# Two head pairs' queries transposed by a DMA instead of TensorE, one copy for two pairs' keys, and a new order of work beside the units

## The chip, the cores and the metric

The kernel runs on one core of one Trainium2 chip. The metric is the device time of one execution in microseconds; several executions are timed and the median is given. One further execution is recorded by the hardware profiler.

## The reference

Inputs are q, k and v of shape (8 sequences, 8 heads, 576 positions, 64), a small position network (w1, b1, w2), and a mixture of eight experts.

```python
scores = q @ k^T / 8 + bias[h]            # per sequence and head; bias depends on position and head alone
attn   = exp(scores - max);  attn /= attn.sum(-1) + 1e-9
x      = attn @ v                          # -> (8*576 tokens, 512)
for e in range(8):                         # every token belongs to one expert (moe_domain_id)
    out[tokens of e] = relu(x[tokens of e] @ w1[e]) @ w2[e]     # 512 -> 1024 -> 512
```

## The kernel before, in words

**Stages.** A first stage evaluates the position network and leaves exp(bias) tables in SBUF (`_phase_bias`, nine blocks `ib` = 0 to 8). A second does the attention of the eight sequences (`_Attention.run`) and scatters the rows of x, sorted by expert, to a scratch tensor `fire_x` in HBM. A third runs the experts (`_phase_moe`). At the start of the first stage one SP DMA fills `fire_x` with zeros (line 277, 9252 KB).

**Attention of one sequence.** Scores are computed with the keys on the partitions. The eight heads are four pairs p = 0 to 3. A sequence has 21 *units*, each some matmuls into a PSUM tile `sc` (two buffers) and one exponential on ScalarE (`L593`) from there to SBUF: unit 0 `("r", 0)` and unit 9 `("r", 1)` hold the last 64 keys of pairs 0, 1 and of pairs 2, 3; units 1 to 8 the 512 main keys of pairs 0 and 1; 10 to 13 those of pair 2; 14, 15 the last 64 queries; 16 is a small corner (256 columns); 17 to 20 the main keys of pair 3. Unit 20 and its like add the bias by a matmul (`L561`); the others are multiplied by the exp(bias) tables on VectorE.

**Beside the units.** TensorE, VectorE and ScalarE each run in the order in which the program is written (`manual_schedule`). `PLAN` is that order: slot n of the list is put behind unit n. `A p c` is one group of attention-times-value matmuls of pair p (p = 4 is the last 64 queries) into the one PSUM tile `pu`; `N p` normalizes `pu` on VectorE (a reciprocal and a multiply) and must end before the next pair's first `A`; `W n` multiplies unit n's exponentials by their table; `V` copies v beside its columns of ones; `T p q` and `T p k` are eight TensorE transposes each for the next sequence's q and k of pair p into a PSUM tile `pt` (p = 4: the last 64 rows, four each); `D p` copies that tile to SBUF on VectorE. A prime means that the work belongs to the preceding sequence. `PLAN0` is the same list for sequence 0.

**Loads.** GpSimd issues the loads of q, k and v (float32 in HBM, float16 in SBUF) two sequences ahead, in a fixed order with the scatters (`G.issue`); `n4` is a ring of six buffers for them. q and k lie as [128, 8 heads, 4 rows, 64]: partition i holds positions 4i to 4i+3. SP issues the zero fill, the experts' transposing reads of `fire_x` (lines 830 and 993, `dma_start_transpose`) and their staged weights (786); its order is the tile framework's.

**Sequence 0.** Pairs 2 and 3 of sequence 0 are transposed after units 4 and 5 and copied out of PSUM by ScalarE (`L533`), one copy each. Behind unit 7 stand the transposes of the last 64 rows of sequence 1 (`T4q`, `T4k`, tile `last`).

**Into the experts.** When the first seven sequences are scattered, SP issues a transposing read `xA` of the first 512 rows of expert 0 (line 993). TensorE's first expert matmul (`L851`) stands behind the last `A` group of sequence 7.

Of the kernel before, what the change touches and what calls it, by code (L numbers as in the profile page):

```python
# [40 lines left out]
W4 = C4 + S  # L41
# [8 lines left out]


PLAN = (
    "A40' A41' A42'",
    "W19' A43' A44' A45' V",
    "A46' A47' W0",
    "T0q T0k N4'",
    "T4q W2 D0 A30' A31'",
    "A32' A33' A34'",
    "A35' A36' A37' W4",
    "T1q T4k",  # L60
    "N3' A00 A01 A02 D4",
    "W6 A03 W8 A04",
    "A05 A06 A07",
    "T2q",
    "T1k N0 A10",
    "W9 A11 A12 W11",
    "A13 A14 D1 A15",
    "A16 A17",
    "W13",
    "T2k N1",  # L70
    "D2 A20 A21 A22 A23 A24 A25 A26 A27 W15 N2",
    "",
    "T3q W18 T3k D3",
)

PLAN0 = [" ".join(t for t in slot.split() if t not in ("T0q", "T0k", "T4q", "D0")) for slot in PLAN]
# [21 lines left out]

def _ins(inst):
    return inst.ins if hasattr(inst, "ins") else inst  # L100


class _Issue:
# [94 lines left out]
def _phase_bias(tc, G, route, at, x_dram):  # L198


    nc = tc.nc
    with tc.tile_pool(name="fsb", bufs=1, side="right") as fsb, \
# [67 lines left out]
        for ib in range(9):  # L270
            if ib == 7:
                at.transposes(0, 1)
            after = hidden(ib + 1) if ib < 8 else None
            if ib == 1:
                G.last_table()
                nc.vector.memset(G.zero.rearrange("p o (r d) -> p (o r) d", r=4)[:, :, DM:].bitcast(I32), PAD)
                nc.sync.dma_start(out=x_dram.rearrange("(p c r) d -> p c (r d)", p=P, r=4),
                                  in_=G.zero.to_broadcast([P, NSLOT // P // 4, 4 * XW]))
            if ib == 5:
                at.transposes(0, 4)  # L280
                at.transposes(0, 0)
            if ib == 8:
                for ui in range(HEAD):
                    at.unit(0, ui, fps.tile([P, 2, 512], F32, tag="eb", name="eb", bufs=3))
            outputs(ib, hrl)
            if ib == 0:
                next(route)
            if ib == 8:
                at.weight(at.jobs.pop((0, 0)))
                at.make_vext(0)  # L290
                for k in range(7):
                    if k == 3:
                        at.weight(at.jobs.pop((0, 2)))
                    next(route)
            hrl = after
# [134 lines left out]
class _Attention:  # L430
# [10 lines left out]
    def __init__(self, tc, G, q, k, v, x_dram):  # L441
        self.tc, self.nc, self.G = tc, tc.nc, G
        self.q, self.k, self.v, self.x_dram = q, k, v, x_dram
        self.nat, self.vst, self.qkT, self.qkTl, self.e, self.xt, self.xl, self.pt = ({} for _ in range(8))
# [24 lines left out]
    def load_qk(self, b, xs="qk"):  # L469
        nc = self.nc  # L470
        for nm in xs:
            src = self.q if nm == "q" else self.k
            t = self.G.n4(nm + "n").rearrange("p (h r d) -> p h r d", r=4, d=D)
            self.G.issue(nc.gpsimd.dma_start(out=t, in_=src[b, :, 0:512, :]
                                        .rearrange("h (p r) d -> p h r d", r=4)))
            self.nat[b, nm] = t

    def load_last(self, b, xs="qk"):
        nc = self.nc
# [28 lines left out]
    def transposes(self, b, p, xs="qk"):  # L508

        G = self.G  # L510
        if "q" in xs:
            self.pt[b, p] = G.tps.tile([P, 2, 512] if p < 4 else [P, 4, 2, 128], F16, tag="tr",
                                       name="pt" if p < 4 else "ptl", bufs=2)
        pt = self.pt[b, p]
        for nm in xs:
            x = "qk".index(nm)
            for r in range(4):
                if p < 4:
                    for h2 in range(2):
                        self._transpose(pt[64 * h2: 64 * h2 + 64, x, 128 * r: 128 * r + 128],  # L520
                                        self.nat[b, nm][:, 2 * p + h2, r, :], 128)
                else:
                    self._transpose(pt[:, r, x, :], self.last[b % 2][:, r, x, :], 128)

    def take(self, b, p, eng=None):
        if p < 4:
            t = self.qkT[b, p] = self.G.asb.tile([P, 2, 512], F16, tag="qkT", name="qkT", bufs=8)
        else:
            t = self.qkTl[b] = self.G.asb.tile([P, 4, 2, 128], F16, tag="qkTl", name="qkTl", bufs=2)
        if eng is None:  # L530
            self.nc.vector.tensor_copy(out=t, in_=self.pt.pop((b, p)))
        else:
            eng.copy(out=t, in_=self.pt.pop((b, p)))  # L533

    def unit(self, b, ui, sc=None):
        self.jobs[b, ui] = self.scores(b, self.units[ui], sc)

    def scores(self, b, u, sc=None):
        nc, G = self.nc, self.G
        mm = nc.tensor.matmul  # L540
# [15 lines left out]
        if u[0] == "m":  # L556
# [4 lines left out]
                    mm(out=sc[:, h2, :], lhsT=G.idn, rhs=G.biasW[c][:, 2 * p + h2 - RAW[c], :],  # L561
                       start=True, stop=False)
            for h2 in range(2):
                mm(out=sc[:, h2, :], lhsT=self.qkT[b, p][hs[h2], 1, 128 * c: 128 * c + 128],  # L564
                   rhs=self.qkT[b, p][hs[h2], 0, :], start=not raw, stop=True)
            c0 = c if j is None else c - 1
            bias = None if raw else G.biasM[:, c0: c + 1, 2 * p: 2 * p + 2, :].rearrange("p c h i -> p c (h i)")
        elif u[0] == "r":
            for p in range(2):
                mm(out=sc[:, p, :], lhsT=self.qkTl[b][:, 2 * u[1] + p, 1, :],  # L570
                   rhs=self.qkT[b, 2 * u[1] + p][:, 0, :], start=True, stop=True)
            bias = G.biasR[:, 2 * u[1]: 2 * u[1] + 2, :].rearrange("p q i -> p (q i)")
        elif u[0] == "l":
            for lj in range(2):
                c = 2 * u[1] + lj
                for p in range(4):
                    mm(out=sc[:, lj, :].rearrange("k (h p q) -> k h p q", h=2, p=4)[:, :, p, :],
                       lhsT=self.qkT[b, p][:, 1, 128 * c: 128 * c + 128],
                       rhs=self.qkTl[b][:, p, 0, :].rearrange("k (h q) -> k h q", h=2),
                       start=True, stop=True)  # L580
# [12 lines left out]
        nc.scalar.activation(out=ef[:, 0:n], in_=sf[:, 0:n], func=AF.Exp, bias=0.0, scale=0.125)  # L593
        if bias is None or j == 0:
            return None
        if j == 1:
# [95 lines left out]
    def run(self, route, late):  # L692
# [338 lines left out]
```

## Time and profile before

| | us |
|---|---|
| time, median of 3 runs (lowest to highest) | 355.24 (354.95 to 355.83) |
| the profiled execution's own time | 355.02 |
| its span, first to last instruction | 353.5 |
| TensorE matmul busy in the span | 324.5 (92%) |
| VectorE busy | 247.3 (70%) |
| ScalarE busy | 246.3 (70%) |
| GpSimd busy | 167.7 (47%) |

The span lacks some 1.5 us of the execution's own time. The busy shares are means over three stages: the position network to about 50 us, attention to about 207 us, the experts behind it. A matmul's end is modelled, so a busy TensorE may also be waiting inside a group. Two neighbouring instructions' records overlap a little, so a pace is read from start to start.

### The profile page before, as it was taken

The numbers are of one execution on the slowest core, as the hardware profiler recorded it, in microseconds if no ns is written. First come the engines' busy times: TensorE is split into PE (matmuls) and PEld (weight loads), VectorE is DVE, ScalarE is ACT, GpSimd is POOL, SyncE is SP. The second block draws the span as 40 slices with busy tenths as digits, with TensorE's granted clock in tenths as the row PEclk, the third lists the DMA queues.
The fourth block names the chain that finished last, engine by engine and source line by source line (L and its number), as shares of the span: only waits on it lengthen the run. The fifth ranks groups of instructions, "written<-read, shape, count | busy, mean of one in ns | idle before, by whom it ended". The sixth has DMA issues, their size and how long they took to land. (4 is left out here: it accounts for less than half of the span.)

```text
span 353.5 us, 9881 instructions
## 1 busy us (share of the span) xinstructions
PE 324.5 (92%) x4218; PEld 213.4 (60%) x4218; DVE 247.3 (70%) x436; ACT 246.3 (70%) x299; POOL 167.7 (47%) x211
## 2 busy tenths in 40 slices
PE   0489888999999999999999899999999999999993
PEld 0478855766666676666675564565655555565651
DVE  7999998999999999999999861206163616161211
ACT  7999989999999999999999953241424232323330
POOL 8370004727687676958483622506051515151323
PEclk9999757999999999999999999999999999999998
DMA  3999999999999899999999543999999999980202
GB/s 43 195 158 345 352 341 213 192 194 163 167 128 192 115 190 111 200 101 200 149 202 220 129 71 93 283 323 230 322 206 325 248 289 264 271 322 32 114 32 107
DMA packets 89349, 69.20 MB, mean 196 GB/s; under 512 B 43605, under 2 KB 77653, under 8 KB 89304
## 3 DMA queue, kind: packets, MB, share of 16 engines
q0 software_dynamic: 51984, 37.26, 65.0%
q1 hardware_dynamic: 37320, 31.30, 32.7%
q8 instruction: 33, 0.54, 0.6%
q14 instruction: 12, 0.10, 0.1%
HBM read 61.93 MB, written 24.70 MB: 245 GB/s over the span
## 5 line engine op out<-in xcount | busy, mean ns | idle before, releaser
L593 ACT ACTIVATE e<-sc 128x1024 f16<-128x1024 f32 x157 | 148.2, 1059 | 1.7
L874 ACT ACTIVATE hT<-hps 128x640 f16<-128x640 f32 x56 | 39.4, 704 | 78.1 <-PE hps L841 77.8
L820 DVE COPY res<-ops 128x512 f32<-128x512 f32 x39 | 27.0, 692 | 91.1 <-PE ops L813 90.1
L821 POOL DMA_INDIRECT out_dram<-res,ids x40 | 44.9, 1123 | 89.8 <-DVE res L820 73.3
L604 DVE TENSOR_TENSOR e<-e,biasM 128x2048 f16<-128x2048 f16 x64 | 72.9, 1149 | 1.6 <-ACT e L593 1.5
L813 PE MATMUL ops<-w,hT 128*128 128x512 f16 x320 | 70.5, 379 | 0.0
L629 PE MATMUL pu<-vext,e 128*128 128x65 f16 (+1 forms) x1280 | 64.8, 194 | 0.0
L841 PE MATMUL hps<-xT,w 128*128 128x320 f16 x448 | 62.0, 299 | 0.0
L629 PEld LDWEIGHTS <-e 128*128 128x128 f16 (+1 forms) x1280 | 56.1, 101 | 8.8 <-issue 6.8
L841 PEld LDWEIGHTS <-w 128*128 128x128 f16 x448 | 43.8, 98 | 18.1
L813 PEld LDWEIGHTS <-hT 128*128 128x128 f16 x320 | 31.2, 98 | 36.5 <-ACT hT L853 0.3
L564 PE MATMUL sc<-qkT 64*128 64x512 f16 x252 | 49.7, 391 | 3.8 <-ACT e L593 3.6
L671 POOL DMA_INDIRECT fire_x<-xt,posi x32 | 40.1, 1253 | 15.3 <-issue 7.6
L218 DVE TENSOR_SCALAR hr<-L,slope,nb 128x576 f16<-128x576 f16 x113 | 41.4, 433 | 0.1
L238 PE MATMUL eb<-W2BIG,hr 128*128 128x32 f16 x576 | 24.0, 192 | 14.6 <-DVE W2BIG L187 10.1
L627 PE MATMUL pu<-vrag,e 128*128 128x130 f16 (+1 forms) x160 | 35.7, 223 | 0.2 <-ACT e L593 0.2
L238 PEld LDWEIGHTS <-hr 128*128 128x128 f16 x576 | 21.5, 115 | 17.8 <-POOL vrag L450 6.7
L215 ACT ACTIVATE hr<-L,pb,slope 128x576 f16<-128x576 f16 x31 | 24.6, 873 | 1.4 <-DVE nb L183 1.2
L671 POOL DMA_INDIRECT fire_x<-xl,posi x8 | 9.1, 1133 | 30.8 <-issue 13.8
L564 PEld LDWEIGHTS <-qkT 64*128 64x128 f16 x256 | 13.5, 93 | 16.3 <-issue 8.3
L643 DVE TENSOR_TENSOR xt<-pu,rz 128x512 f16<-128x512 f32 (+1 forms) x33 | 22.3, 675 | 1.5
L627 PEld LDWEIGHTS <-e 128*128 128x128 f16 (+1 forms) x160 | 16.0, 100 | 11.2 <-issue 6.6
(124 smaller groups left out, 352.5 us busy)
## 6 DMA issues: line engine op xcount, KB each, us to landing
st<-in_moe_w_dram SPq DMA_DIRECT2D x15, 1024.0 KB
fire_x<-zero SPq DMA_DIRECT2D x1, 9252.0 KB
w<-in_moe_w_dram POOLq DMA_DIRECT2D x17, 512.0 KB
qn<-in_q_dram POOLq DMA_DIRECT2D x8, 512.0 KB
kn<-in_k_dram POOLq DMA_DIRECT2D x8, 512.0 KB
vst<-in_v_dram POOLq DMA_DIRECT2D x8, 512.0 KB
out_dram<-res,ids POOLq DMA_INDIRECT x40
last<-zero SPq DMA_DIRECT2D x2, 256.0 KB
```

The costliest lines, as they stand in the source:

```text
L218: nc.vector.tensor_scalar(out=hr, in0=G.L4[:, c0: c0 + S], scalar1=G.slope[:, m: m + 1], scalar2=G.nb1[:], op0=AO.mult, op1=AO.max)
L238: nc.tensor.matmul(out=eb[:, lj, 32 * k16: 32 * k16 + 32], lhsT=rap(hr, jc, [[4, 128]]), rhs=G.W2BIG[:, 0:32], start=True, stop=True)
L564: mm(out=sc[:, h2, :], lhsT=self.qkT[b, p][hs[h2], 1, 128 * c: 128 * c + 128], rhs=self.qkT[b, p][hs[h2], 0, :], start=not raw, stop=True)
L593: nc.scalar.activation(out=ef[:, 0:n], in_=sf[:, 0:n], func=AF.Exp, bias=0.0, scale=0.125)
L604: self.nc.vector.tensor_tensor(out=job[0], in0=job[0], in1=job[1], op=AO.mult)
L627: mm(out=out, lhsT=last, rhs=vr[:, pair, :], start=True, stop=False, skip_group_check=True)
L629: mm(out=out[:, 65 * h2: 65 * h2 + 65], lhsT=keys[j], rhs=vx[:, 2 * pair + h2, j, :], start=False, stop=(h2 == 1 and j == 3), skip_group_c ...
L671: inst = self.nc.gpsimd.indirect_dma_start(out=self.x_dram[:, :], out_offset=bass.IndirectOffsetOnAxis(ap=self.G.posi[0:n, c:c + 1], axis= ...
L813: nc.tensor.matmul(out=ops_, lhsT=hT[:, fc, t0: t0 + 128], rhs=G.w.w2(e, fc), start=(fc == 0), stop=(fc == 7))
L821: inst = nc.gpsimd.indirect_dma_start(out=out[:], out_offset=bass.IndirectOffsetOnAxis(ap=idx.bitcast(I32), axis=0), in_=res[:], in_offset ...
L841: nc.tensor.matmul(out=hps[:, i, 0:HC], lhsT=G.w.w1(e, dc, fc), rhs=xT[:, dc, HC * hf: HC * hf + HC], start=(dc == 0), stop=(dc == 3))
L874: nc.scalar.activation(out=hT[:, fc, :].rearrange("p (a b) -> p a b", a=2), in_=first(e, xT, ((fc, 0), (fc, 1))), func=AF.Relu, bias=0.0, ...
```

## The change

`load_qk` loads q in two DMAs: heads 0 to 3 into the first half of the buffer as before, and heads 4 to 7 into its second half, `natx`, a [128, 1024] block. A new function `cross` issues one transposing DMA on SP from `natx` to a new tile `qx` (two buffers). For sequence 0 it is called in block 4 of the first stage without a further wait; for sequence b + 1 it is called behind unit 4 of sequence b and waits, by a semaphore (`_behind`), for that unit's exponential. The transposes `T2q` and `T3q` are gone; `T2k` and `T3k` write the two halves of one PSUM tile, and one copy `D2` moves both (`D3` is gone). In sequence 0 one ScalarE copy stands behind unit 4 where two stood behind units 4 and 5. The matmuls take q of pairs 2 and 3 from `qx` and k of both from one tile. `PLAN` is dealt anew.

```diff
-    "A40' A41' A42'",            "W19' A43' A44' A45' V",     "A46' A47' W0",
-    "T0q T0k N4'",               "T4q W2 D0 A30' A31'",       "A32' A33' A34'",
-    "A35' A36' A37' W4",         "T1q T4k",                   "N3' A00 A01 A02 D4",
-    "W6 A03 W8 A04",             "A05 A06 A07",               "T2q",
-    "T1k N0 A10",                "W9 A11 A12 W11",            "A13 A14 D1 A15",
-    "A16 A17",                   "W13",                       "T2k N1",
-    "D2 A20 A21 A22 A23 A24 A25 A26 A27 W15 N2",  "",         "T3q W18 T3k D3",
+    "W18' A40' A41' A42' V T0q", "A43' A44' A45' W0",         "A46' A47' W19'",
+    "N4' T0k",                   "W2 A30' A31' T4q",          "D0 A32' A33' A34'",
+    "A35' W4 A36' A37'",         "T4k T1q",                   "N3' A00 W6 D4 A01",
+    "A02 A03 A04 W8",            "W9 A05 A06",                "A07 N0 T2k",
+    "T1k",                       "A10 A11 A12",               "A13 A14 D1 W11 A15",
+    "W13 A16 A17 N1",            "",                          "T3k D2",
+    "A20 W15 A21 A22 A23 A24 A25",  "A26 A27",                "N2",
...
+            if ib == 4:
+                at.cross(0)
...
-            t = self.G.n4(nm + "n").rearrange("p (h r d) -> p h r d", r=4, d=D)
-            self.G.issue(nc.gpsimd.dma_start(out=t, in_=src[b, :, 0:512, :]
+            src = (self.q if nm == "q" else self.k)[b, :, 0:512, :]
+            t = self.G.n4(nm + "n")
+            n = 1024 if nm == "q" else 2048
+            self.nat[b, nm] = t[:, 0:n].rearrange("p (h r d) -> p h r d", r=4, d=D)
+            self.G.issue(nc.gpsimd.dma_start(out=self.nat[b, nm], in_=src[0: n // 256]
                                         .rearrange("h (p r) d -> p h r d", r=4)))
+            if nm == "q":
+                self.natx[b] = t[:, n:]
+                self.G.issue(nc.gpsimd.dma_start(out=t[:, n:].rearrange("p (r h d) -> p r h d", r=4, d=D),
+                                                 in_=src[4:].rearrange("h (p r) d -> p h r d", r=4)))
+    def cross(self, b, behind=None):
+        self.qx[b] = self.G.asb.tile([P, 4, 2, 128], F16, tag="qx", name="qx", bufs=2)
+        inst = self.nc.sync.dma_start_transpose(out=self.qx[b].rearrange("p r a i -> p (r a) i"),
+                                                in_=self.natx.pop(b))
+        if behind is not None:
+            _behind(self.tc, inst, behind)
...
-            if b == 0 and ui in (4, 5):
-                self.transposes(0, ui - 2)
-                self.take(0, ui - 2, self.nc.scalar)
+            if b == 0 and ui == 4:
+                self.transposes(0, 2, "k")
+                self.transposes(0, 3, "k")
+                self.take(0, 2, self.nc.scalar)
+            if ui == 4 and b < B - 1:
+                self.cross(b + 1, self.exps)
```

(The lists are shown here three slots to a line, slot 0 first.)

## Rows read from the trace of the kernel before

**Rows 1.** Busy time in a window: PE, PEld, DVE, ACT, POOL, clock, DMA share, GB/s.
```profile
131.01:150.03 19.02, 18.77 (x317) 12.76 (x318) 18.64 (x28) 18.86 (x21) 14.32 (x18) 1.00 1.13 157
```

**Rows 2.** Timeline of ACT, sequence 4 to sequence 5: start, length, what, count.
```profile
131.96 7.44 ACT L593 ACTIVATE e<-sc 128x1024 f16<-128x1024 f32 x8
...
138.30 7.52 ACT L593 ACTIVATE e<-sc 128x1024 f16<-128x1024 f32 x8
...
145.63 0.47 ACT L593 ACTIVATE e<-scx 128x256 f16<-128x256 f32 x1
145.89 4.07 ACT L593 ACTIVATE e<-sc 128x1024 f16<-128x1024 f32 x4
...
150.03 1.02 ACT L593 ACTIVATE e<-sc 128x1024 f16<-128x1024 f32 x1
```

**Rows 3.** Timeline of PE, units 18 to 20 of sequence 4.
```profile
146.22 0.23 PE L627 MATMUL pu<-vrag,e 128*128 128x130 f16 x1
...
147.58 0.39 PE L564 MATMUL sc<-qkT 64*128 64x512 f16 x2
...
148.82 0.41 PE L505 MATMUL pt<-idn,qn 128*64 128x128 f16 x8
...
149.39 0.60 PE L570 MATMUL sc<-qkT,qkTl 128*128 128x512 f16 x2
```

**Rows 4.** Timeline of DVE: a copy from PSUM and the next instruction.
```profile
135.32 0.68 DVE L531 COPY qkT<-pt 128x1024 f16<-128x1024 f16 x1
135.92 1.21 DVE L604 TENSOR_TENSOR e<-e,biasM 128x2048 f16<-128x2048 f16 x1
```

**Rows 5.** Timeline of ACT, sequence 0, units 5 and 6 with the second copy.
```profile
57.85 1.06 ACT L593 ACTIVATE e<-sc 128x1024 f16<-128x1024 f32 x1
58.76 1.05 ACT L533 COPY qkT<-pt 128x1024 f16<-128x1024 f16 x1
59.65 1.08 ACT L593 ACTIVATE e<-sc 128x1024 f16<-128x1024 f32 x1
```

**Rows 6.** Timeline of PE, sequence 0, units 7 to 9; idle time and its end in brackets.
```profile
61.04 0.38 PE L505 MATMUL ptl<-idn,last 128*128 128x128 f16 x4 [0.37 <-DMA last<-in_k_dram]
61.35 0.39 PE L564 MATMUL sc<-qkT 64*128 64x512 f16 x2
...
62.19 0.59 PE L570 MATMUL sc<-qkT,qkTl 128*128 128x512 f16 x2
```

**Rows 7.** Timeline of SP: DMAs issued, and how long each issue took.
```profile
5.62 1.31 SPq L455 DMA_DIRECT2D last<-zero  x2
7.03 2.62 SPq L452 DMA_DIRECT2D vrag<-vrag  x2
...
21.89 0.60 SPq L277 DMA_DIRECT2D fire_x<-zero  x1
...
203.08 2.59 SPq L993 DMA_TRANSPOSE xA<-fire_x  x1
...
221.97 1.82 SPq L786 DMA_DIRECT2D st<-in_moe_w_dram  x3
223.83 13.74 SPq L830 DMA_TRANSPOSE xT<-fire_x  x1
```

**Rows 8.** Busy time in windows of sequence 4, columns as in Rows 1.
```profile
137.00:138.50 1.50, 1.50 (x26) 0.93 (x25) 1.47 (x4) 1.50 (x3) 0.41 (x2) 1.00 0.47 28
...
140.00:148.00 8.00, 7.75 (x147) 5.81 (x144) 7.84 (x13) 7.93 (x10) 7.07 (x10) 1.00 1.36 206
```

**Rows 9.** Timeline of POOL: k of a sequence is issued; a later issue waits for its landing.
```profile
122.77 0.89 POOL L474 DMA_DIRECT2D kn<-in_k_dram  x1
...
131.90 0.84 POOL L483 DMA_DIRECT2D last<-in_k_dram  x1 [1.23 <-DMA kn<-in_k_dram]
```

**Rows 10.** Timeline of PE: that k is first transposed.
```profile
133.74 0.39 PE L505 MATMUL pt<-idn,kn 128*64 128x128 f16 x8
```

**Rows 11.** Timeline of PE: the experts' first matmuls.
```profile
208.74 1.24 PE L851 MATMUL hps<-xA,w 128*128 128x512 f16 x5
```

More of the change, by code (lines that the diff above doesn't have):

```diff
@@ L52 @@
 PLAN = (
[L53 to L71, printed above, removed]
-    "",
-    "T3q W18 T3k D3",
+    "W18' A40' A41' A42' V T0q",
+    "A43' A44' A45' W0",
+    "A46' A47' W19'",
+    "N4' T0k",
+    "W2 A30' A31' T4q",
+    "D0 A32' A33' A34'",
+    "A35' W4 A36' A37'",
+    "T4k T1q",
+    "N3' A00 W6 D4 A01",
+    "A02 A03 A04 W8",
+    "W9 A05 A06",
+    "A07 N0 T2k",
+    "T1k",
+    "A10 A11 A12",
+    "A13 A14 D1 W11 A15",
+    "W13 A16 A17 N1",
+    "",
+    "T3k D2",
+    "A20 W15 A21 A22 A23 A24 A25",
+    "A26 A27",
+    "N2",
 )
@@ L100, in _ins, with _behind @@
     return inst.ins if hasattr(inst, "ins") else inst
+def _behind(tc, inst, before):
+    tc.add_manual_dep(_ins(inst), before.name, mybir.DependencyInfo(
+        mybir.DependencyClass.Sync, mybir.DependencyReason.DATA), reason="paced")
 class _Issue:
@@ L443, in __init__ @@
         self.q, self.k, self.v, self.x_dram = q, k, v, x_dram
-        self.nat, self.vst, self.qkT, self.qkTl, self.e, self.xt, self.xl, self.pt = ({} for _ in range(8))
+        self.nat, self.vst, self.qkT, self.qkTl, self.e, self.xt, self.xl, self.pt, self.natx, self.qx = \
+            ({} for _ in range(10))
         nc, asb = self.nc, G.asb
@@ L471, in load_qk @@
         for nm in xs:
-            src = self.q if nm == "q" else self.k
-            t = self.G.n4(nm + "n").rearrange("p (h r d) -> p h r d", r=4, d=D)
-            self.G.issue(nc.gpsimd.dma_start(out=t, in_=src[b, :, 0:512, :]
-                                        .rearrange("h (p r) d -> p h r d", r=4)))
-            self.nat[b, nm] = t
+            src = (self.q if nm == "q" else self.k)[b, :, 0:512, :]
[3 more added lines that the diff above has]
+            self.G.issue(nc.gpsimd.dma_start(out=self.nat[b, nm], in_=src[0: n // 256]
+                                        .rearrange("h (p r) d -> p h r d", r=4)))
+            if nm == "q":
+                self.natx[b] = t[:, n:]
+                self.G.issue(nc.gpsimd.dma_start(out=t[:, n:].rearrange("p (r h d) -> p r h d", r=4, d=D),
+                                                 in_=src[4:].rearrange("h (p r) d -> p r h d", r=4)))
+    def cross(self, b, behind=None):
[4 more added lines that the diff above has]
+            _behind(self.tc, inst, behind)
     def load_last(self, b, xs="qk"):
@@ L510, in transposes @@
         G = self.G
-        if "q" in xs:
+        home = 2 if p == 3 else p
+        if p != 3 and (p == 2 or "q" in xs):
             self.pt[b, p] = G.tps.tile([P, 2, 512] if p < 4 else [P, 4, 2, 128], F16, tag="tr",
                                        name="pt" if p < 4 else "ptl", bufs=2)
-        pt = self.pt[b, p]
+        pt = self.pt[b, home]
         for nm in xs:
-            x = "qk".index(nm)
+            x = "qk".index(nm) if p not in (2, 3) else p - 2
             for r in range(4):
@@ L526, in take @@
         if p < 4:
-            t = self.qkT[b, p] = self.G.asb.tile([P, 2, 512], F16, tag="qkT", name="qkT", bufs=8)
+            t = self.qkT[b, p] = self.G.asb.tile([P, 2, 512], F16, tag="qkT", name="qkT", bufs=6)
         else:
@@ L533, in take, with qT, kT @@
             eng.copy(out=t, in_=self.pt.pop((b, p)))
+    def qT(self, b, p):
+        return (self.qkT[b, p][:, 0, :].rearrange("d (r i) -> d r i", r=4) if p < 2 else
+                self.qx[b][:, :, p - 2, :])
+    def kT(self, b, p):
+        return self.qkT[b, p][:, 1, :] if p < 2 else self.qkT[b, 2][:, p - 2, :]
     def unit(self, b, ui, sc=None):
@@ L563, in scores @@
             for h2 in range(2):
-                mm(out=sc[:, h2, :], lhsT=self.qkT[b, p][hs[h2], 1, 128 * c: 128 * c + 128],
-                   rhs=self.qkT[b, p][hs[h2], 0, :], start=not raw, stop=True)
+                mm(out=sc[:, h2, :].rearrange("k (r i) -> k r i", r=4),
+                   lhsT=self.kT(b, p)[hs[h2], 128 * c: 128 * c + 128],
+                   rhs=self.qT(b, p)[hs[h2]], start=not raw, stop=True)
             c0 = c if j is None else c - 1
@@ L569, in scores @@
             for p in range(2):
-                mm(out=sc[:, p, :], lhsT=self.qkTl[b][:, 2 * u[1] + p, 1, :],
-                   rhs=self.qkT[b, 2 * u[1] + p][:, 0, :], start=True, stop=True)
+                mm(out=sc[:, p, :].rearrange("k (r i) -> k r i", r=4), lhsT=self.qkTl[b][:, 2 * u[1] + p, 1, :],
+                   rhs=self.qT(b, 2 * u[1] + p), start=True, stop=True)
             bias = G.biasR[:, 2 * u[1]: 2 * u[1] + 2, :].rearrange("p q i -> p (q i)")
@@ L577, in scores @@
                     mm(out=sc[:, lj, :].rearrange("k (h p q) -> k h p q", h=2, p=4)[:, :, p, :],
-                       lhsT=self.qkT[b, p][:, 1, 128 * c: 128 * c + 128],
+                       lhsT=self.kT(b, p)[:, 128 * c: 128 * c + 128],
                        rhs=self.qkTl[b][:, p, 0, :].rearrange("k (h q) -> k h q", h=2),
@@ L592, in scores @@
         ef, sf = e.rearrange("p a i -> p (a i)"), sc.rearrange("p a i -> p (a i)")
-        nc.scalar.activation(out=ef[:, 0:n], in_=sf[:, 0:n], func=AF.Exp, bias=0.0, scale=0.125)
+        self.exps = _ins(nc.scalar.activation(out=ef[:, 0:n], in_=sf[:, 0:n], func=AF.Exp, bias=0.0, scale=0.125))
         if bias is None or j == 0:
```

## The prediction

> **What bounds the kernel now.** I read the busy time by stage first, then the timeline of ScalarE (ACT) by units, then what TensorE (PE) and VectorE (DVE) do where ACT is late. In one sequence of attention, 19.02 us, PE, DVE and ACT are busy 18.77, 18.64 and 18.86 us [rows 1]: the busy shares name nobody, so a pace is needed. Between units 1 and 8 ACT starts seven exponentials in 138.30 - 131.96 = 6.34 us, 0.906 each [rows 2]. The reader is to see that this is ACT's own pace, each record of about one us reaching into the next. At that pace a sequence is 20 x 0.906 + 0.26 (the narrow unit 16, 145.63 to 145.89) = 18.38 us. It takes 19.02, so 0.64 is lost. The place shows in the same rows: units 17 to 20 and the step to the next unit 0 take 150.03 - 145.89 = 4.14 for four where 3.62 is the pace; 0.52 is lost there, 0.12 elsewhere.
>
> There PE is late: the eight groups A20 to A27 stand in one slot, 146.22 to 147.58, and only then come unit 19's scores; behind unit 20 stand T3q and T3k, 148.82 to 149.39, ahead of unit 0's scores [rows 3]. `sc` has two buffers, so PE can be ahead of ACT by less than two units; 1.36 us in one slot is more than that cover gives.
>
> **The change part by part.**
>
> *q transposes off PE.* Sixteen transposes a sequence go. T3q and T3k together are sixteen in 0.57 us [rows 3], so 0.57 us of PE work goes per sequence. Most units hide that; it counts only where PE is late, between units 17 and 20.
>
> *New deal.* The eight A2 groups are cut into six and two. A pair of groups is 1.36 / 4 = 0.34, so slot 18 has 1.02 and slot 19 0.34 us on PE instead of 1.36 and nothing. Unit 18's scores (I take 0.35, a little under the record of 0.39 for unit 19's [rows 3]) may start when unit 15's exponential ends, that is with unit 16's, 0.26 before unit 17's; T3k, 0.29, now stands ahead of them and has room behind unit 17's scores, which may start a whole unit earlier. Counted from unit 17's exponential, unit 18's scores end at 0.09, the six groups at 1.11; unit 19's scores are wanted at 1.81. Those and unit 20's take 148.82 - 147.58 = 1.24 with the wait that is now among them [rows 3], slot 19 takes 0.34: 2.69, against 2.72 when ACT wants unit 20. It just fits, without T3q or T3k behind it. So the 0.52 should go, and the 0.12 with it for the most part.
>
> *One copy less on DVE.* A copy occupies DVE for 135.92 - 135.32 = 0.60 us [rows 4]. DVE's 18.64 busy becomes 18.04 against ACT's 18.38. What is late next is DVE: 0.34 us of slack in a sequence, and it runs in order, with N3 ahead of A00 and N1 ahead of A20 because `pu` is a single buffer. I leave a tenth of the gain for that.
>
> *Sum over the sequences.* The loss at units 17 to 20 is there in all eight: 8 x 0.52 = 4.2. The other 0.12 counts in sequences 1 to 6: 0.7. Together 4.9, less a tenth: 4.4. Its bounds are 0 (DVE takes over all of it) and 4.9.
>
> *Sequence 0: one ACT copy less.* The second copy takes ACT from 58.76 to 59.65, 0.89 us [rows 5]. I give nothing for it, because of what is late next: behind unit 7 PE already waits 0.37 us for the landing of sequence 1's last k rows, at 61.04 [rows 6]. Reaching that point earlier only makes the wait longer. In the new slot T1q stands behind the wait instead of ahead of it, some 0.3 us, before unit 8's scores, which began at 61.35 [rows 6]. And the load itself now stands behind two further q loads, each an issue like that of k, 0.89 us [rows 9]: it lands 0 to 1.8 later; I take 0.5, nearer to 0, because the bytes are the same. Price 0.8; bounds: a gain of 0.89, if the rows land earlier, and a loss of 0.3 + 1.8 = 2.1.
>
> *The transposing DMAs.* For them the trace has `xA`: 512 rows x 512, issued at 203.08 with an issue of 2.59 [rows 7], read by PE at 208.74 [rows 11], so at most 5.66 us. Each new one is half as large: at most 2.8 and no less than nothing. Issued behind unit 4, it is wanted at unit 9 of the next sequence, 26 units or some 23 us later. That wait holds up only what is behind it on SP, and until the experts this is only the next of its kind, and `xA`. Its packets fall where the DMA engines are nearly idle: 0.47 busy at 137.0 to 138.5, just after unit 4 (about 134.7 to 135.7), against 1.36 at 140 to 148 [rows 8]. Cost taken: nothing. If the cover is gone, the loads behind are late (third rival).
>
> *The extra load issue.* GpSimd is busy 14.32 of 19.02 [rows 1]; 0.9 more leaves it 3 us. Nothing is taken.
>
> *The tail.* Behind the last exponential both plans have the same PE work and the same order on DVE (N2, W18, W19, N4), so the experts begin the same distance behind attention, and their own stage is untouched. `xA` hangs on N3 of sequence 6, which stays in slot 8. Nothing gained or lost.
>
> Sum: 4.4 - 0.8 = 3.6 us. The profiled execution took 355.02 (353.5 of span and 1.5 around it, which nothing here touches); less 3.6 that is 351.4. The median of the runs is 0.22 above that execution, so I predict 351.6 us.
>
> **The rivals.**
>
> *DVE takes over.* ACT's lateness at units 17 to 20 moves to where PE waits for N3 or N1. For it: 0.34 us of slack is thin for an in-order engine that also waits for each `A` to end. Against it: when it has work queued it does not idle. At half of the gain, 2.45 - 0.8 = 1.65: 353.6; at none of it 356.0.
>
> *The first transposing DMA comes behind the zero fill.* `cross(0)` stands behind the fill in the code, both go out on SP, and the fill's 9.25 MB were issued at 21.89 and still slow the loads that land at 61.04 [rows 6, 7]. A transposing read issued behind three staged weight loads took 13.74 us to issue, against 2.59 alone [rows 7]. If the fill is gone at about 60 to 62, where the load beside it lands, and with 2.6 + 2.8 us for issue and transfer at the most, q of pairs 2 and 3 is there between 62.8 and 67.4; unit 9's scores want it at 62.19 + 0.8 = 63.0 [rows 6]. So 0 to 4.4 us of standstill on PE, middle 2.2: 353.8. Against it: SP's order isn't that of the code. The two `last` copies of line 455 went out before the `vrag` copies of line 452 [rows 7], as if what is ready first went first, and q of sequence 0 is among the first loads. The Trainium skill, "DMA: Bandwidth & Descriptors", Queues, rings and completion order, has it that an engine takes one ring's descriptors in ring order and goes round between rings packet by packet; by that rule the DMA would stand behind the whole fill if issued after it, and this rival would be sure given the order. The 13.74 us agree.
>
> *The loads of k come too late (slower).* k of a sequence is issued at 122.77 and has landed by 131.90 [rows 9]; T0k reads it at 133.74 [rows 10]: 1.84 us of margin. The shorter sequence takes 0.64 of it, the extra issue 0.89, leaving 0.3; up to 2.8 us of transposing packets would make it up to 2.5 late, in six sequences. It decides the sign from 0.6 late (6 x 0.6 = 3.6); at 1.2 late the time is 351.6 + 7.2 = 358.8. Against it: the idle DMA stretch [rows 8], and PE's own cover of about half a unit. The same page of the Trainium skill, Latency and other measured facts, gives 261 GB/s for a transposing DMA; 256 KB would then be some 1.0 us, an estimate by that figure, with which k would be 0.7 late at most. No run here shows that rate for a source in SBUF.
>
> *Nothing eats the copy's 0.89 in sequence 0*: 351.6 - 0.8 - 0.9 = 349.9.
>
> **How the numbers follow.** Forecast 0.56, its own range 350.5 to 352.7. DVE takes over 0.18, behind the fill 0.12, k too late 0.09, nothing eaten 0.05. The range for 8 in 10 runs from 349.8 to 355.0: it leaves out the slower rival and the far ends of the first two. What can be told from no change is about 0.3%, 1.07 us. Faster takes the forecast, the last rival, three quarters of DVE and of the fill: 0.83, less 0.03 for what I have not seen: 0.80. Same: 0.08, most of the rest of these two. Slower: 0.12.
>
> **What would show it.** Right: from unit 17 to the next unit 0 about 3.65 us instead of 4.14; a sequence 18.4 to 18.5; one copy `qkT<-pt` fewer in each; PE in sequence 0 waiting 1 us or more for `last<-in_k_dram` behind unit 7; the experts' first matmul near 205. Wrong: idle PE ahead of unit 9's scores in sequence 0 with a transposing DMA as its end (the fill); PE idle ahead of A00 or A20 by `xt` (DVE); idle ahead of T0k by a landing of `kn` (k too late). A sequence at 18.4 with the total still near 355 would put the error into sequence 0 or the tail.

## The result: 359.76 us, slower, and the profile after

The changed kernel takes 359.76 us (358.97 to 360.71, 4 runs) beside 355.53 (354.95 to 356.34, 4 runs) of the kernel before: ratio 1.0118, with a 95% interval of 1.0080 to 1.0157 (the numbers in brackets behind a ratio below are such intervals). Forecast were 351.6 us and a range of 349.8 to 355.0; both were wrong, and so was the sign.

One line of the diff stands wrong ahead of the prediction. The kernel's new load reads `in_=src[4:].rearrange("h (p r) d -> p r h d", r=4)`; the text there has `"... -> p h r d"`. Its pieces, contiguous on both sides, are 64 elements of one row (128 bytes written), 2048 of them, where the other loads of the first 512 rows of q, k and v write pieces of 256 elements (512 bytes). I read the load as one like those. The experiments below show what that cost.

The spans of the profiled executions, cut at the first and the last exponential of attention (us):

| | before | after | e1: wide pieces | forecast of the change |
|---|---|---|---|---|
| first exponential | 49.89 | 53.62 | 50.07 | 0 |
| from it to the last | 156.10 | 157.08 | 154.63 | -3.6 |
| from the last to the end | 147.48 | 148.39 | 147.78 | 0 |
| span | 353.46 | 359.10 | 352.49 | -3.6 |

Of the 5.6 us lost, 3.7 are gone before attention begins, where the forecast has nothing. (The profiled execution of the kernel after, 360.71 us, is the slowest of its four; the medians are 4.2 us apart.) The page of the kernel after (span, busy times, packets, and the first stage's VectorE group: busy us, mean ns):

```profile
span 359.1 us, 9652 instructions
...
PE 323.7 (90%) x4090; PEld 211.4 (59%) x4090; DVE 248.4 (69%) x429; ACT 246.3 (69%) x298; POOL 178.4 (50%) x219
...
DMA packets 110211, 71.27 MB, mean 198 GB/s; under 512 B 68565, under 2 KB 98517, under 8 KB 110168
...
L223 DVE TENSOR_SCALAR hr<-L,slope,nb 128x576 f16<-128x576 f16 x113 | 45.1, 469 | 0.1
```

and the same lines of the kernel before:

```profile
DMA packets 89349, 69.20 MB, mean 196 GB/s; under 512 B 43605, under 2 KB 77653, under 8 KB 89304
...
L218 DVE TENSOR_SCALAR hr<-L,slope,nb 128x576 f16<-128x576 f16 x113 | 41.4, 433 | 0.1
```

The reader is to see two things: 25,000 more packets under 512 bytes for 2 MB more moved (8 x 2048 = 16,384 of them are the new load's; the rest is in e1 below too, where that load has large pieces), and 113 instructions that nobody edited taking 3.7 us more. Where they take it, the timeline of VectorE (start, length, what, count) shows at two places, before:

```profile
5.79 2.96 DVE L218 TENSOR_SCALAR hr<-L,slope,nb 128x576 f16<-128x576 f16 x6
...
18.77 3.07 DVE L218 TENSOR_SCALAR hr<-L,slope,nb 128x576 f16<-128x576 f16 x8
```

and after:

```profile
5.79 4.23 DVE L223 TENSOR_SCALAR hr<-L,slope,nb 128x576 f16<-128x576 f16 x6
...
20.33 4.71 DVE L223 TENSOR_SCALAR hr<-L,slope,nb 128x576 f16<-128x576 f16 x8
```

GpSimd's timeline of the kernel after has the new load at just these places, and 1.6 and 2 times as long as the load of q's first half, 0.95 and 0.75:

```profile
6.56 1.56 POOL L488 DMA_DIRECT2D qn<-in_q_dram  x1
...
21.33 1.48 POOL L488 DMA_DIRECT2D qn<-in_q_dram  x1 [3.11 <-DMA vst<-in_v_dram]
```

(The bracket is idle time ahead of an instruction and what ended it.) A single tensor_scalar takes 1.24 us at 7.02 and 1.26 at 21.68 instead of about 0.42, and the two behind it 0.95 to 0.97; a third such load at 47.67 stretches one to 1.28.

In attention a sequence of the steady state answers to [rows 1] and [rows 2] thus (busy times in a window; then ScalarE's starts):

```profile
154.06:172.97 18.91, 18.61 (x304) 12.56 (x302) 18.26 (x27) 18.86 (x23) 15.57 (x20) 1.00 1.28 169
```

```profile
153.14 15.79 ACT L623 ACTIVATE e<-sc 128x1024 f16<-128x1024 f32 x17
168.81 0.39 ACT L623 ACTIVATE e<-scx 128x256 f16<-128x256 f32 x1
169.08 4.91 ACT L623 ACTIVATE e<-sc 128x1024 f16<-128x1024 f32 x5
```

From unit 17 (169.08) to the next unit 0 (172.97) it takes 3.89 us: 4.14 before, 3.65 forecast. VectorE's busy time falls from 18.64 to 18.26 as intended; GpSimd's rises from 14.32 to 15.57, and the DMA share from 1.13 to 1.28. And two sequences are longer than the rest: sequence 2 takes 20.61 us, and sequence 7 18.66 from its first to its last exponential, against 17.92 before.

### The profile page after: what moved, and what is told of

It is laid out like the page before. It is cut to its first block, busy times and chain, and to the rows that moved or that the text cites. A ratio compares the mean times of both kernels' runs of the same rounds, so it can differ in the third digit from the quotient of the medians.

```text
span 359.1 us, 9652 instructions
## 1 busy us (share of the span) xinstructions
PE 323.7 (90%) x4090; PEld 211.4 (59%) x4090; DVE 248.4 (69%) x429; ACT 246.3 (69%) x298; POOL 178.4 (50%) x219
## 5 line engine op out<-in xcount | busy, mean ns | idle before, releaser
L223 DVE TENSOR_SCALAR hr<-L,slope,nb 128x576 f16<-128x576 f16 x113 | 45.1, 469 | 0.1
L243 PE MATMUL eb<-W2BIG,hr 128*128 128x32 f16 x576 | 24.8, 193 | 17.1 <-DVE W2BIG L192 11.3
L593 PE MATMUL sc<-qx,qkT 64*128 64x512 f16 x128 | 25.0, 384 | 3.1 <-ACT e L623 2.3
L593 PE MATMUL sc<-qkT 64*128 64x512 f16 x124 | 25.3, 402 | 1.8 <-ACT e L623 1.3
L593 PEld LDWEIGHTS <-qkT 64*128 64x128 f16 x256 | 14.5, 93 | 18.8 <-issue 9.8
```

What stands on the lines that cost most here:

```text
L223: nc.vector.tensor_scalar(out=hr, in0=G.L4[:, c0: c0 + S], scalar1=G.slope[:, m: m + 1], scalar2=G.nb1[:], op0=AO.mult, op1=AO.max)
L243: nc.tensor.matmul(out=eb[:, lj, 32 * k16: 32 * k16 + 32], lhsT=rap(hr, jc, [[4, 128]]), rhs=G.W2BIG[:, 0:32], start=True, stop=True)
L593: mm(out=sc[:, h2, :].rearrange("k (r i) -> k r i", r=4), lhsT=self.kT(b, p)[hs[h2], 128 * c: 128 * c + 128], rhs=self.qT(b, p)[hs[h2]], s ...
```

## The experiments

Times are medians, beside runs of the kernel before on the same chip: 354.86 us for e1 to e4, 354.71 for e5 to e8, 355.46 for e9 to e12. e1 to e8 ran on one chip, e9 to e12 on another; which chip the kernel after ran on is not on record. In e1, e5, e7, e9, e10 and e12 rows of q are mixed up in some or all sequences; the work is the same.

Theory A was formed from the two timelines above: pieces of 64 elements that GpSimd writes while VectorE works hold VectorE up. Its rival: the deal, the transposing DMAs or the number of packets cost the time.

**e1, the pieces made wide.**

```diff
-  out=t[:, n:].rearrange("p (r h d) -> p r h d", ...), in_=src[4:].rearrange("h (p r) d -> p r h d", r=4)
+  out=t[:, n:].rearrange("p (h r d) -> p h r d", ...), in_=src[4:].rearrange("h (p r) d -> p h r d", r=4)
```

> The changed kernel with one edit: heads 4 to 7 of q land in pieces of 256 elements (in the order head, row) as the other loads do, instead of pieces of 64 (row, head); so pairs 2 and 3 get rows of q that belong elsewhere, and nothing else changes. Theory A (the 64-element pieces: GpSimd writes four times as many descriptors, VectorE stands still meanwhile in the first stage, and the load queue fills): the first exponential returns from 53.6 to 50.0 to 50.7 us and the time to 354.0 to 356.0. Theory B (the transposing DMAs themselves, or the order on SP, cost it): first exponential stays at 53 or later, time 358 to 360.

Measured: 354.15 us (12 runs), ratio 0.9981 (0.9968 to 0.9995). First exponential at 50.07. Against its own runs of before it stands at -0.7 us, the kernel after at +4.2: this one line of the load is worth 4.9 us, as far as two kernels that were not timed side by side tell. The load takes 0.84 us of GpSimd, and VectorE's stretch at 5.79 is back below that of before, here as e1's GpSimd and VectorE timelines have it:

```profile
6.56 0.84 POOL L488 DMA_DIRECT2D qn<-in_q_dram  x1
```

```profile
5.79 2.64 DVE L223 TENSOR_SCALAR hr<-L,slope,nb 128x576 f16<-128x576 f16 x6
```

**e2, the kernel before with that load and nothing else of the change.** Line of the diff: as the added load above, in the old `load_qk`.

> The kernel before with one part of the change alone: heads 4 to 7 of q loaded by a DMA of their own in 64-element pieces; TensorE still transposes all of it. Theory A: the first exponential moves from 49.9 to 53 to 54 us and the time from 355.5 to 358.5 to 360.5. Theory B: both stay, 355 to 356.

Measured: 358.16 us, ratio 1.0098 (1.0071 to 1.0125); first exponential at 54.41, 4.5 later than before, and from it to the last 156.18 us, as before (156.10). The load alone makes the kernel before slower, and nearly all of it ahead of attention. Not all of the 4.5 us is VectorE's: its last tensor_scalar starts 2.28 later than before (53.70 for 51.42). Some 2 us more are a pause of TensorE, which is in both kernels at one place of the program but not of one length. TensorE before:

```profile
44.96 0.25 PE L238 MATMUL eb<-W2BIG,hr 128*128 128x32 f16 x2
45.82 0.75 PE L238 MATMUL eb<-W2BIG,hr 128*128 128x32 f16 x10 [0.61 <-DVE hr L218]
```

and in e2:

```profile
47.44 0.83 PE L238 MATMUL eb<-W2BIG,hr 128*128 128x32 f16 x20
50.87 0.50 PE L238 MATMUL eb<-W2BIG,hr 128*128 128x32 f16 x10 [2.60 <-DVE hr L218]
```

The brackets name VectorE, but in e2 VectorE's last tile of that block ended at 48.89 and ScalarE's at 49.32 at the latest. The pause is 1.17 us in the kernel after and 1.50 in e1, so it is not what tells those two apart. In both traces the queue for instructions has a transfer of 16 KB there, 43.51 to 44.39 before and 48.35 to 49.23 in e2. That TensorE waits for instructions fits this; it wasn't tested.

**e3, the first three sequences on the old path** (PE transposes for sequences 0 to 2, whose q is loaded wide; the rest as after):

```diff
...
+ OLD = 3
+ def _old(slot):
+     return slot.replace("N0 T2k", "N0 T2q T2k").replace("T3k D2", "D2 T3q T3k").replace("N2", "N2 D3")
...
```

> The changed kernel, but sequences 0 to 2, whose q is loaded before attention, take q of pairs 2 and 3 as before: one load in 256-element pieces, TensorE transposes, a copy per pair. The narrow loads and the transposing DMA begin with sequence 3. Theory A: first exponential at 49.8 to 50.5, time 353.8 to 355.5. Theory B: the later sequences still pay, 356.5 to 358.5.

Measured: 362.15 us, ratio 1.0191 (1.0168 to 1.0214). A miss, with the first exponential at 50.45 where it should be. Its trace is of its slowest execution, 365.48 us. Three causes appear in it: the end of the program, which e5 shows by itself; waits for v's last rows, 0.50 us in sequence 6 and 4.34 in sequence 7; and in sequence 1, which has all its transposes in the new order, 19.78 us, as e4 has it in every sequence.

**e4, the new deal alone**, with all transposes and copies of before (`OLD = 8`).

> The new order of work alone: all eight sequences loaded, transposed and copied as before (T2q beside T2k, T3q beside T3k, D2 and D3), in the new list of slots. My prediction's step (six and two A2 groups fit under ScalarE's pace): the step from unit 17 to the next unit 0 shrinks from 4.14 to 3.7 to 3.9, the time to 353.5 to 354.5. Rival, from the trace of the changed kernel (scores reach ScalarE some 0.6 us after they start, so TensorE has next to no lead): the loss only moves to other units, a sequence 18.9 to 19.3 us, time 355 to 357.

Measured: 360.46 us, ratio 1.0174 (1.0151 to 1.0198): a sequence takes 19.85 us, 0.83 more than with the old deal. It loses 0.36 at units 17 to 18, 0.47 at 18 to 19, 0.27 at 19 to 20. Without the removed transposes the new deal is a loss.

**e5 and e10, pieces of 64 elements in one part of the sequences only.** e5 has them from sequence 3 on, e10 in sequences 0 to 2:

```diff
+  o = "p h r d" if b < 3 else "p r h d"      # e5; e10: b >= 3
```

> The kernel after, with the second half of q loaded in 256-element pieces for sequences 0 to 2 (whose loads are issued in the first stage and at the start of attention; their rows of pairs 2 and 3 are mixed up by that) and in 64-element pieces for sequences 3 to 7. Theory A (64-element pieces cost time only while GpSimd writes them beside the first stage's tensor_scalars on VectorE): first exponential at 50.1 us, 354.0 to 355.0 us, as with all pieces wide (354.15). Rival B (four times the pieces also hold up the later loads, above all v's last rows): the first exponential at 50.1 too, but waits of the A00 matmuls for v's last rows in sequences 3 to 7 of 0.5 us or more, and 355.5 to 358 us.

> The mirror of e5: 64-element pieces for sequences 0 to 2 and 256-element pieces for sequences 3 to 7 (their rows of pairs 2 and 3 are mixed up by that). Theory A (64-element pieces written by GpSimd beside the first stage's tensor_scalars hold up VectorE): the first exponential 3.0 to 4.6 us later than with all pieces wide (50.07), the rest as there, 357.4 to 358.8 us. Rival B (the price of the kernel after is spread over all its loads): the first exponential before 52 us, 355.5 to 356.8 us.

Measured: e5 359.07 us, ratio 1.0134 (1.0088 to 1.0181); e10 363.84, ratio 1.0239 (1.0201 to 1.0277). Both totals are misses, but of the first stage both say the same as e1 and e2. The instructions of VectorE's group (count; min, median and longest ns; first and last start), e5:

```profile
L223 DVE TENSOR_SCALAR hr<-L,slope,nb x113: 399/420/666, 5.8 to 51.1; 128x576 f16<-128x576 f16 x113
```

and e10:

```profile
L223 DVE TENSOR_SCALAR hr<-L,slope,nb x113: 398/416/1398, 5.8 to 55.2; 128x576 f16<-128x576 f16 x113
```

With the small pieces of sequences 0 to 2 the first exponential is at 53.66, without them at 50.32; the kernel after has 53.62, e1 50.07. e12 below, on e10's chip and with large pieces there, has 50.34. So 3.3 to 3.6 us of the loss are these three loads. TensorE's granted clock is not the cause: from 44 to 56 us it was at the lower of its two levels, 1.2 GHz, in the kernels before, after and e10, and at 2.4 GHz in e1, e2, e5 and e12, and each level has early and late first exponentials (before 49.89, e2 54.41). In e5 attention itself takes 154.64, as with all pieces wide (154.63): from sequence 3 on the pieces cost nothing there, though T0k waits for k 0.65 us at 95.54 and 0.40 at 152.19. e5 loses its 4 us behind the last landing. GpSimd's last scatter and the span, e5:

```profile
348.26 0.98 POOL L856 DMA_INDIRECT out_dram<-res,ids  x1 [0.87 <-POOLq L936]
```

```profile
span 356.9 us, 9652 instructions
```

and e1:

```profile
348.01 0.98 POOL L854 DMA_INDIRECT out_dram<-res,ids  x1 [0.88 <-POOLq L934]
```

```profile
span 352.5 us, 9652 instructions
```

The same last instruction, 0.25 us later, and an end 4.4 us later: GpSimd's closing drain, an instruction at the program's end, takes 5.70 us instead of 2.56, and its semaphore instruction ahead of that 1.57 instead of 0.59; from 350.4 us on no DMA moves bytes.

**e12, the pieces from sequence 4 on**, to see whether that drain goes by their number:

```diff
+  o = "p h r d" if b < 4 else "p r h d"
```

> As e5, with 64-element pieces for sequences 4 to 7 only (rows of pairs 2 and 3 of sequences 0 to 3 are mixed up by that). In e5 the attention took what it takes with wide pieces, but GpSimd's closing drain took 5.70 us instead of 2.56, and its last semaphore instruction 1.57 instead of 0.59. Theory E (the closing drain grows with the 64-element pieces of the late loads): four such loads, 4.5 to 5.7 us of drain, 357 to 358.5 us. Rival F (it depends on where GpSimd's writing of descriptors happens to end, not on their number; the kernel after, with eight such loads, has 2.85): 2.5 to 2.9 us of drain, 354.0 to 355.0 us.

Measured: 359.76 us, ratio 1.0101 (1.0071 to 1.0131). The drain takes 4.48; the time lies above both ranges, for the reason that e9 shows below. With e10's 4.89 the order is: no such load 2.56, three 4.89, four 4.48, five 5.70 (e3 too), all eight 2.85. It does not go by number; the kernels in which this load changes its form between sequences have the long one. Why, is open.

**e6, small pieces that GpSimd doesn't write.** q is loaded wide and put in order by SP:

```diff
+  qy = asb.tile([P, 4, 4, D], F16, ...)
+  for h in range(4):
+      inst = self.nc.sync.dma_start(out=qy[:, :, h, :], in_=nat[:, h])
+      if behind is not None and h == 0:
+          _behind(self.tc, inst, behind)
...
-      in_=self.natx.pop(b))
+      in_=qy.rearrange("p r h d -> p (r h d)"))
```

> The kernel after, with the second half of q loaded in 256-element pieces and put into the order that the transposing DMA wants by four SBUF-to-SBUF DMAs of SP (512 pieces of 128 bytes each), issued where the transposing DMA was. The pieces of 128 bytes are as many as in the kernel after, but GpSimd doesn't write them. Theory A (GpSimd's writing of them beside VectorE is what costs): first exponential at 50.1 us, 354.0 to 355.0 us. Rival B (the number of small pieces in the DMA engines costs, whoever issues them): first exponential past 51.5 us or waits for q of the last pairs, v's last rows or k, 356.5 to 360 us.

Measured: 370.21 us, ratio 1.0348 (1.0304 to 1.0393). VectorE is not held up (first exponential at 49.87; SP issues such DMAs at 13.62 and 34.27, and no tensor_scalar takes more than 0.67), as theory A has it, but waits as in the rival are there, and dearer than thought. TensorE waits for the transfers (two places of many):

```profile
85.95 1.03 PE L604 MATMUL sc<-qx,qkTl 128*128 128x512 f16 x2 [4.83 <-DMA qx<-qy]
...
108.22 0.27 PE L661 MATMUL pu<-vrag,e 128*128 128x130 f16 x1 [2.39 <-DMA vrag<-in_v_dram]
```

v's last rows take 8 to 11 us from issue to landing in attention, 6 to 9 in e1. The 16 us more than e1 are not the price of the small pieces alone: only the first of the four DMAs waits for unit 4, so that those of sequence 1 go out early and the zero fill behind them, at 37.42 instead of 21.5; four DMAs stand ahead of each transposing one; and behind the first wait shown the granted clock is 0.50, from 85 to 90 us, after 5 us in which TensorE was busy for 1.12.

**e7, the old deal with the transposes removed** (wide pieces):

```diff
-    "T2q",                    "D2 A20 ... A27 W15 N2",      "T3q W18 T3k D3",
+    "",                       "A20 ... A27 W15 N2",         "W18 T3k D2",
```

> The kernel with all pieces 256 elements wide (rows of pairs 2 and 3 mixed up), q of the last two pairs by the transposing DMA, but the deal of the kernel before, less its two transposes and the copy that fall away (slot 11 empty, slot 20 W18 T3k D2). Theory D1 (the gain is TensorE's removed transposes, the new deal adds nothing): the loss at units 20 to 21 (0.20) goes, that at 18 to 19 (0.31) stays, 18.82 us a sequence, 353.8 to 354.8 us. Rival D2 (the new deal is what makes the gain): 19.0 us a sequence as before, 355.3 to 356.3 us.

Measured: 353.98 us (12 runs), ratio 0.9986 (0.9966 to 1.0005), beside e1's 0.9981: theory D1. What decides is the trace, for the ratio's interval holds 1: a sequence takes 18.80 us with either deal; the old one loses 0.32 at units 18 to 19, the new one 0.33 at 19 to 20. Most of what the two deals can gain is one and the same 0.2 us.

**e8 and e9, the last rows of q and k of sequence 1 ahead of its v** (e8 on e6, e9 on e7):

```diff
   self.load_qk(b)
+  if b:
+      self.load_last(b)
   self.load_v(b)
```

> The kernel e6 with the last 64 rows of q and k of sequence 1 issued ahead of its v. With all loads wide, sequence 0 loses 1.38 us at units 7 to 8 and 0.47 at 8 to 9, where T4q and T4k wait for these rows, which land at 59.5 to 59.9 us behind v and the zero fill. Theory C (they are late because they queue behind v and beside the fill): they land before 52 us, both losses fall to 0.4 together, and the time is 1.0 to 1.6 us below that of e6. Rival (the next thing is as late: v of sequence 1, q and k of sequence 2): the loss moves to another unit and the time is within 0.4 us of e6.

> The kernel e7 (all pieces 256 elements wide, rows of pairs 2 and 3 mixed up, old deal) with the last 64 rows of q and k of sequence 1 issued ahead of its v, as in e8 but without e8's SBUF-to-SBUF DMAs. e7 loses 1.44 us at units 7 to 8 of sequence 0 and 0.38 at 8 to 9, where T4q and T4k wait for these rows. Theory C (they are late because they queue behind v): both losses together fall below 0.5 and the time is 352.4 to 353.0 us, 1.0 to 1.6 below e7 (353.98). Rival (the next load is as late, or the first stage is held up instead): within 0.4 us of e7.

Measured: e8 368.81 us, ratio 1.0350 (1.0314 to 1.0387); e9 359.38, ratio 1.0097 (1.0060 to 1.0134). e8 does not test theory C, for in e6, on which it stands, these rows land at 34.7 to 35.2 already: what e6 loses at units 7 to 9, 1.19 and 0.60, goes with a granted clock of 0.56 to 0.58 from 56 to 64 us, where e8 has 1.00 and loses 0.39 and nothing. In e9 the loss shrinks to 0.72 and 0.12, for 1.43 and 0.37 in e7, whose clock is lower there too (0.50 and 0.67; e9 1.00). What holds the rows is the zero fill more than v: behind v and fill they land at 58.70 to 59.65 (e7), ahead of v but behind the fill at 53.05 to 57.90 (e9), and with the fill sent at 34 us or later, not at 21, at 34.7 to 35.2 behind v (e6) and 30.3 to 32.4 ahead of it (e8). But the time does not follow. e8 loses the gain ahead of these units: from unit 2 to unit 3, where TensorE pauses for 1.60 us, it takes 1.71 longer than e6, and its first exponential is 1.27 later. e9, each against its own runs of before, is 4.7 us slower than e7, through losses that no wait in its trace explains, at the same unit of sequences 2 to 5. ScalarE in sequence 3 of e9:

```profile
128.27 1.02 ACT L623 ACTIVATE e<-sc 128x1024 f16<-128x1024 f32 x1 [1.34 <-PE sc L593]
```

TensorE's records end these scores at 126.67; ScalarE and VectorE, which waits for TensorE too, both go on 1.6 us later. The clock is granted in full there. The kernel after has the same at 113.94 (1.02 idle) and 205.65 (0.66), with the rows of its ScalarE:

```profile
113.94 2.85 ACT L623 ACTIVATE e<-sc 128x1024 f16<-128x1024 f32 x3 [1.02 <-PE sc L593]
...
205.65 1.94 ACT L623 ACTIVATE e<-sc 128x1024 f16<-128x1024 f32 x2 [0.66 <-PE sc L607]
```

e10, e11 and e12 have such places (e10 some 2.9 us of them in sequences 1 and 2, which with its drain is why it missed), the kernel before, e1, e2, e5 and e7 none. What holds TensorE's signals there is open. The four runs e9 to e12 are also the four on the other chip, so that the chip, and not what these kernels change, may bring the late signals about; no kernel was traced on both.

**e11, the transposing DMAs alone**, added to the kernel before, their result unused:

```diff
+  if ui == 4 and b < B - 1:
+      self.cross(b + 1, self.exps)
```

> The kernel before, all its transposes kept, with the eight transposing DMAs added on SP where the kernel after has them (from the second half of the q tile into a tile that nothing reads). Theory (my prediction's step: these DMAs are hidden): 354.7 to 355.2 us, within 0.3 of before, first exponential within 0.3 us of 49.89. Rival (they hold up the loads behind them or the zero fill): waits for the last rows of q and k or v in sequences 0 and 1, 355.5 to 357 us.

Measured: 355.90 us, ratio 1.0020 (0.9998 to 1.0043): 0.7 us, not told from nothing, and above the theory's range. Half of its 12 runs lie at 355.2 to 355.7, half at 356.1 to 358.5 (five above 357; of the 17 of the kernel before beside them, one); the profiled one, 357.65, has a late signal as above in sequence 1 and 2 us more in all in sequences 0 and 1. From sequence 3 on each takes 19.02, as before.

## Why the prediction was wrong, step by step

**The step that failed** is *The extra load issue*: "0.9 more leaves it 3 us. Nothing is taken." It rests on *Sequence 0*'s "because the bytes are the same". I compared bytes and GpSimd's slack in a steady sequence [rows 1, 9], and did not ask how the bytes are cut, nor what the same load does in the first stage, where VectorE, not TensorE, sets the pace (in the kernel before it is busy all 12 us from 40 to 52). Measured: the issue takes 1.5 us, not 0.9, and three of them put 3.3 to 3.6 us into the first stage (e1 against after, e5 and e12 against e10); e2, with two in that stage, starts its last tensor_scalar there 2.28 later. The clue stood in the kernel before: its tensor_scalars, 418 ns in the median, have a longest one of 776, and 0.67 to 0.70 us at 7.17, 8.09, 19.11 and 22.84, beside GpSimd's load issues.

The Trainium skill, "DMA: Bandwidth & Descriptors", SWDGE vs HWDGE vs iDMA, says that the rings are SBUF state which GpSimd writes while it makes descriptors, and that VectorE locks GpSimd out of it in its two-port modes. The traces show the two in each other's way, in the other direction: VectorE's instruction gets longer.

**New deal and q transposes: 4.4 forecast, 1.44 measured** (e1: sequences 1 to 7 take 130.99, before 132.43). Mis-sized is "counted from unit 17's exponential ... 2.69, against 2.72": I let TensorE's lead run through from unit to unit. TensorE in the kernel after, answering to [rows 3]:

```profile
170.35 0.39 PE L593 MATMUL sc<-qx,qkT 64*128 64x512 f16 x2
170.68 0.23 PE L657 MATMUL pu<-vrag,e 128*128 128x130 f16 x1
170.74 0.42 PE L659 MATMUL pu<-vext,e 128*128 128x65 f16 x8
171.09 0.59 PE L590 MATMUL sc<-biasW,idn 128*128 128x512 f16 x2
171.62 0.39 PE L593 MATMUL sc<-qx,qkT 64*128 64x512 f16 x2
172.05 0.59 PE L600 MATMUL sc<-qkT,qkTl 128*128 128x512 f16 x2
```

Unit 20's scores can't start before unit 19's exponential does, at 170.98, for only then is a buffer of `sc` free; they take from 171.09 to 172.01, and ScalarE, free at 170.98 + 0.90 = 171.88, starts at 172.05. So at this unit there is no lead to spend: 0.17 is lost here and 0.09 a unit earlier. In e1, where 0.33 is lost here alone, the sum fails at its first term. TensorE there:

```profile
163.63 0.41 PE L526 MATMUL pt<-idn,kn 128*64 128x128 f16 x8
163.98 0.39 PE L593 MATMUL sc<-qx,qkT 64*128 64x512 f16 x2
...
166.59 0.39 PE L593 MATMUL sc<-qx,qkT 64*128 64x512 f16 x2
```

Unit 17's exponential starts at 163.95. Unit 18's scores were to start 0.26 before it; they start 0.03 behind it, at 163.98, because T3k runs until then. From there TensorE works without a gap to the end of unit 20's scores, 166.98: 3.00 us (the sum had 2.95), where ScalarE takes three units at 0.906, 2.72. The work was right; the lead was not there. The 0.52 of [rows 2] did not go; it became about 0.3, with either deal.

**One copy less:** right in kind, smaller in size. VectorE's busy time fell by 0.38 a sequence, not by 0.60, and no wait for `xt` before A00 or A20 replaced it in e1 (one for `xl` ahead of A30, 0.35 and 0.23, in two sequences). The rival that VectorE takes over did not happen.

**Sequence 0: a price of 0.8.** With wide pieces nearly nothing: 23.64 for 23.67 us. As foreseen, TensorE waits there for the last rows: in e1 k's land 1.0 us earlier than before (59.91 for 60.90), but q's 4.2 later (59.52 for 55.30), where 0 to 1.8 later was foreseen. e1's TensorE:

```profile
58.88 0.39 PE L593 MATMUL sc<-qkT 64*128 64x512 f16 x2 [0.87 <-DMA last<-in_q_dram]
59.61 1.03 PE L526 MATMUL ptl<-idn,last 128*128 128x128 f16 x8 [0.33 <-DMA last<-in_q_dram]
```

The 1.4 us more that are lost at units 7 to 9 eat what the copy (0.90) and the first units gave. They go with the wait and with the lower clock of those 4 us (60 to 64: 0.64 granted, before 1.00), which the runs do not part: e5 and e6 lose 1.53 and 1.79 there at 0.63 and 0.58 with no such wait, e4 and e8 at 1.00 nothing and 0.39. In the kernel after, with its first stage 3.7 late, the rows are there and this wait doesn't show.

**The transposing DMAs:** no wait for one in the kernel after or e1, and e11 cannot tell their price from nothing. Their size was wrong: "at most 2.8" us is 3.6 to 9.1 from issue to landing for the first five in the kernel after; the cover of 23 us was enough for that. **Behind the zero fill:** it went out first, at 14.53, the fill at 25.09, and landed at 23.67; SP's order was not the code's. **k too late:** TensorE never stood at T0k in the kernel after (a weight load there was held by less than 0.1 us); in e5 it did, 0.65 and 0.40, without a loss in the sum of attention. Its price, 358.8, was near the result by another mechanism, which is no merit. v's last rows came late instead, in sequence 2 by 1.1 us:

```profile
103.35 0.22 PE L657 MATMUL pu<-vrag,e 128*128 128x130 f16 x1 [1.13 <-DVE e L634]
```

(the bracket names VectorE, but that load landed at 103.10). In sequence 1, where it was issued, GpSimd ran later behind a 1.5 us load, and the expert weights ahead of it took 9.7 us to land, from 92.92 to 102.58, where e1's took 7.6.

**The tail:** "nothing" was 0.9: 0.5 in GpSimd's closing drain and its semaphore instruction, 0.2 behind them, 0.2 in the experts' stage.

**What stays open.** Of 5.6 us, 3.3 to 3.6 are shown as the first three loads and 0.5 lies in the closing drain and the instruction ahead of it. Against e1, attention lost another 2.45 us: 1.8 in sequence 2 (v's last rows and a late signal), 0.8 in sequence 7 (a late signal), 0.8 spread over sequences 3 to 6, less 0.9 gained in sequence 0; e5, with the same loads from sequence 3 on, lost none of it. That the small pieces bring it about is not shown, and the chip is a rival that these runs do not settle. How GpSimd's issue holds VectorE up is not shown either, only that it does so where GpSimd issues small pieces and not where SP does.

No kernel here beats the one before with q in its right order: the gain of e1 and e7, 0.5 to 0.7 us (e7's not told from nothing), would need q in a layout that here only small pieces gave.

## What to carry to other kernels

Before an extra load is called free, count its pieces, contiguous on both sides, and look at what the engines do at each time that it will be issued, not only in the steady state. An engine's lead at a unit is what the trace shows it to be there, and at most what the buffer that it waits for allows; a sum over several units that starts from a lead read off the plan overstates what a new order can win. Try the one line that changes the layout by itself first: here it decided the sign, and the deal and the transposes on which the thought went were worth a fifth of a per cent.

## What the runs showed that I had not expected

- A load issue of 2048 pieces on GpSimd (1.5 us) stretches a VectorE tensor_scalar beside it from 0.42 to 1.24 to 1.40 us; beside the loads in 512-byte pieces the longest is 0.67 in e1 and 0.79 in any run. The 128x2048 tensor_tensors beside the same loads in attention kept their 1.22 us.
- GpSimd's closing drain took 2.55 to 2.85 us in kernels whose q loads have the same form in all sequences, and 4.48 to 5.70 in the four in which the form changes. Why is open.
- Putting q in order by SBUF-to-SBUF DMAs of 128-byte pieces, 2048 in a sequence, cost 16 us (e6 against e1), in transfers that came late and in the lower clock behind them; it moved the zero fill too.
- Late signals of TensorE, 0.5 to 1.6 us each at full granted clock, in the kernel after and in all four runs on the other chip. e9, 4.7 us slower than e7, loses by them in sequences 1 to 5; that its one change, four small loads issued ahead of a large one, brings them about is not shown.
